# Half-swapped copies in place of the second frequency products, and a re-planned order, in a gated mixing kernel

## The chip, the cores and the metric

The kernel runs on one core of one Trainium2 chip. A core has a matrix engine (TensorE, PE in the profile; its weight loads are listed as PEld), three engines for elementwise work (VectorE or DVE, ScalarE or ACT, GpSimd or POOL), a queue engine (SP), and DMA. SBUF is the working memory, PSUM the small memory that PE writes its products to. The metric is the device time of one execution in microseconds (us); before the change it is 467.32 us, the median of three runs.

## The reference

For x of 2048 rows and 640 columns the result is a mix of two branches with a gate per row:

```python
g = sigmoid((x * gate_w).sum(-1, keepdims=True))
# a: 32 heads of 20; each row attends to itself and to 7 rows before it, 2 apart; output projection wo
a = attention(x @ wqkv) @ wo
# b: filter in the frequency plane
X = rfft2(x) * (w_r + 1j * w_i)
b = irfft2(X, s=(2048, 640))
return g * a + (1 - g) * b
```

All arithmetic is in float32.

## The kernel before, in words

Row s is stored as s = 16 p + j: partition p, chunk j (0 to 15). All even chunks need only even chunks in the attention, and all odd chunks only odd ones, since the window goes in steps of 2. So the attention has two halves (`par` 0 and 1).

The work is done in this order, as far as data and buffers force it:

1. `qkv`: eight blocks (two halves, four head groups). Operands are split into a rounded high part and a rest, and three products (high-high, high-rest, rest-high) are summed. Results go to DRAM (`qkvd`). `load_w` and `load_x` load and split the operands: ACT makes the high part, DVE or POOL the rest.
2. `fold` and `cols`: x is folded by symmetry on DVE (tiles `fx`, `fe`), part of it stored in DRAM (`fd`) and loaded again, and PE makes a transform over the 128 partitions into `zg`.
3. `attend`: for each half and head pair group, DVE multiplies keys with queries (`pr`; the queries come from a PSUM bank, `qbank`, filled by ACT) and reduces to logits `L`; ACT takes exponentials; POOL multiplies with values (`pv`); DVE reduces them to `o`, which goes to DRAM.
4. `freq`: 16 groups `g` of frequencies, three or four in flight. ACT copies columns of `zg` to `zc`; PE transforms the columns to `v` and `u`; DVE makes their sum and difference `ab`; PE turns `ab` to the rows at positive frequencies (`xa`, `xb`) and at negative ones (`xc`, `xd`). A product is complex, its real part in partitions 0 to 63 and its imaginary part in 64 to 127. `xb` and `xd` are the same numbers as `xa` and `xc` multiplied by i: the halves exchanged, one with its sign turned. They are made by a second product with another slice of the table (`mm`). ACT copies `xa`, `xb` to `X`; POOL multiplies with the weights `wp` into `P`; DVE multiplies `xc` and `xd` with theirs (`p`, `xd`) and forms sum and difference `s`; PE transforms back (`g`), and ACT writes the result into `zg`. The four x tiles of a group take the PSUM banks 3 and 4 in turn (`BX`).
5. `project_even`: for each even chunk, transposes (`oTp`), 30 products with `wo` (`woa`, `wob`), scaling with the gate on ACT (`ya`), and a store to DRAM (`ad`).
6. `spatial`: for each chunk the inverse transform (`oa`, `ob`, `ha`, `hb`), unfolded on DVE; even chunks add `ad` on POOL and go out.
7. `project_odd`: for each odd chunk the unfolding (`ye`, `y`), transposes, 30 products, and the output.

The code does not issue instructions as it goes. `Plan.record` notes each operation with its engine, and `Plan.cost` gives it a duration. `Plan.touch` finds dependences: a PSUM bank counts as one region, and two operations on a region depend on each other when one of them writes. `Plan.order` simulates all five queues many times, forward by priority and backward from due times, moves the priorities at random, and keeps the order with the smallest simulated end, averaged over draws with late loads (`late`). `Plan.issue` then issues everything in that order, so each engine's and each queue's order is fixed. Input loads get an earliest time (`op.early`), counted back from the simulated end with the constant `AHEAD`. Every recorded operation carries the line of the helper that replays it, 636, so groups are told apart by their tiles.

Of the kernel before, what the change touches and what calls it, by code (L numbers as in the profile page):

```python
# [141 lines left out]
class Op:  # L142
    __slots__ = ("i", "eng", "name", "call", "busy", "lat", "size", "preds", "succs", "chain", "tail", "start", "end", "early", "group", "of", "two")
# [12 lines left out]
class Plan:  # L156
# [31 lines left out]
    def touch(self, op, ap, write):  # L188
# [14 lines left out]
        for pg in np.unique(idx // size):  # L203
            mine = idx[idx // size == pg]
            lo, hi, dense = mine[0], mine[-1], len(mine) == mine[-1] - mine[0] + 1
            kept = []
            for acc in pages.get(pg, ()):
                o, w, q0, q1, alo, ahi, adense, aidx = acc
                hit = o is not op and q0 < p1 and p0 < q1 and alo <= hi and lo <= ahi
                if hit and not (dense and adense):  # L210
                    hit = len(np.intersect1d(mine, aidx, assume_unique=True)) > 0
                if hit and (w or write):
                    op.preds.add(o)
                covered = write and hit and p0 <= q0 and q1 <= p1
                if covered:
                    covered = lo <= alo and ahi <= hi if dense else len(np.setdiff1d(aidx, mine, assume_unique=True)) == 0
                if not covered:
                    kept.append(acc)
            kept.append((op, write, p0, p1, lo, hi, dense, mine))
            pages[pg] = kept  # L220

    def record(self, eng, name, fn, a, k):
        op = Op()
        op.i, op.eng, op.name, op.chain, op.group = len(self.ops), eng, name, self.chain, self.group
        op.preds, op.succs, op.size, op.early, op.two = set(), [], 0, False, False
# [7 lines left out]
        ins = [v for v in aps if v is not out]  # L233
# [7 lines left out]
    def cost(self, op, out, ins, k):  # L241
# [5 lines left out]
        elif op.eng == "PE":  # L247
            n = int(np.prod(out.shape[1:]))
            if op.name == "transpose":
                op.busy = 0.109  # L250
            elif ins[-1].dtype == F32R:
                op.busy = n / 2400 + 0.018
            else:
                op.busy = 4 * n / 2400 + 0.006
            op.lat = 0.25
        elif op.eng == "DVE":
            op.busy, op.lat = 0.075 + n / 960, 0.12
            two = sum(v.tensor.tag[:4] not in ("bank", "qban") for v in ins) == 2
            if op.name == "scalar_tensor_tensor":
                op.busy += 0.06  # L260
            elif op.name == "reciprocal":
                op.busy += n * 0.007
            elif two:
                op.two = True
        elif op.eng == "ACT":
            strided = any(len(v.ap) > 2 and v.ap[-1][0] > 1 for v in [out] + ins)
            op.busy, op.lat = 0.12 + n * (1.75e-3 if strided else 0.78e-3), 0.15
            if len(ins) > 1:
                op.busy += 0.1
        else:  # L270
            spread = any(v.ap[-1][0] == 0 for v in ins)
            op.busy, op.lat = 0.09 + n * (2e-3 if spread else 2.25e-3), 0.14
        if op.eng in ("DVE", "ACT", "POOL") and not op.size:
            op.busy *= PACE

    def order(self):
# [17 lines left out]
        for op in ops:  # L294
            op.early = max(0.0, span - op.tail - AHEAD) if op.early else 0.0
# [3 lines left out]
        best = self.turns(TURNS)  # L299

        names = {n: i for i, n in enumerate(dict.fromkeys(op.of for op in ops))}
        family = np.array([names[op.of] for op in ops])
        for _ in range(AGAIN):
            move = MOVE * rng.choice([0.3, 1.0, 2.0]) * rng.normal(size=len(names))
            move *= rng.random(len(names)) < rng.choice([0.1, 0.5, 1.0])
            for op, t in zip(ops, (best[1] + move[family]).tolist()):
                op.tail = t
# [21 lines left out]
    def late(self, order, draw):  # L329

        line = {e: [op for op in order if op.eng == e] for e in ENGS}
        at, free, rings, link = dict.fromkeys(ENGS, 0), dict.fromkeys(ENGS, 0.0), dict.fromkeys(ENGS, 0.0), 0.0
# [3 lines left out]
        for _ in range(len(order)):  # L336
            for e in ENGS:
                if head.get(e) is None and at[e] < len(line[e]):
                    op = line[e][at[e]]
                    t = free[e]  # L340
                    for q in op.preds:
                        if q not in out:
                            break
                        t = max(t, over[q] if q.eng == e and not q.size else out[q])
# [9 lines left out]
            if op.size:  # L354
                link = max(link, end) + op.size / RATE
                own = rings[e] = max(rings[e], end) + op.size / QUEUE
                end = (own if own >= link else min(link, own + op.size / QUEUE)) + SOONEST + LATER_BY * late
# [53 lines left out]
    def forward(self):  # L411
# [4 lines left out]
        free, rings, link = dict.fromkeys(ENGS, 0.0), dict.fromkeys(ENGS, 0.0), 0.0  # L416
# [5 lines left out]
        while len(done) < len(ops):  # L422
# [28 lines left out]
            if op.size:  # L451
                link = max(link, op.end) + op.size / RATE
                own = rings[e] = max(rings[e], op.end) + op.size / QUEUE
                avail = own if own >= link else min(link, own + op.size / QUEUE)
# [48 lines left out]
class Mixer:  # L503
# [364 lines left out]
    def freq(self, g):  # L868
# [58 lines left out]
        z, sz = col("xc", 1, 0), col("xd", 1, 1)  # L927
# [202 lines left out]

def build(tc, ins, out):
# [45 lines left out]
```

## Time and profile before

| | |
|---|---|
| median of 3 runs (lowest, highest) | 467.32 us (467.08, 467.43) |
| span of the profiled execution, first to last instruction | 465.3 us; its own time is not listed, the median is 2.0 us above the span |
| PE busy | 457.0 us, 98% of the span |
| DVE busy | 423.4 us, 91% |
| POOL busy | 323.9 us, 70% |
| ACT busy | 205.2 us, 44% |
| granted clock of PE | 1.00 in all stretches |

Busy means that an engine had an instruction under way. A group row names the tile written, the tiles read, the shapes and the count; then busy time and mean duration; then idle time of the engine before these instructions, and what ended it. A row of waits gives who waited for whom, the time in total, how often, and the longest. The chain is followed back from the last instruction, at each step to what released it. A float32 product of 321 columns is two matmul instructions in the profile.

### The profile page before, as it was taken

To read this page: it belongs to the slowest core of one execution; us is meant where nothing else is said; L and a number is where in the kernel's file an instruction comes from. 1 tells how busy PE (TensorE), PEld (TensorE's weight loads), DVE (VectorE), ACT (ScalarE), POOL (GpSimd) and SP (SyncE) were. 2 spreads that over 40 slices of the span, in tenths; PEclk is the share of its full clock that TensorE was granted. 3 is DMA by queue.
4 is the path that set the end of the run, shared out by engine and by line. 5 is a ranking of instruction groups with operands and counts; after the bars stand their busy time and mean duration, and the time that the engine had idled before them with its cause. 6 is when DMAs were issued, how large, how long until landed. Compare 5 with 4: busy or idle time off the path is not lost.

```text
span 465.3 us, 7240 instructions
## 1 busy us (share of the span) xinstructions
PE 457.0 (98%) x2497; PEld 399.5 (86%) x2497; DVE 423.4 (91%) x555; ACT 205.2 (44%) x539; POOL 323.9 (70%) x264
## 2 busy tenths in 40 slices
PE   7999999999999999999999999999999999999997
PEld 4788888888889888899887788898888999988996
DVE  4699959999999999998999999999999997989784
ACT  5523346533335453257356465545444564333110
POOL 1003847999999879988698996767877997952300
PEclk9999999999999999999999999999999999999999
DMA  8999998796877968959998466567543321447732
GB/s 310 403 376 308 393 381 314 230 299 197 242 216 252 322 187 275 282 167 276 343 258 307 135 217 220 185 183 234 182 129 120 103 80 56 136 141 220 227 113 85
DMA packets 71700, 105.90 MB, mean 228 GB/s; under 512 B 20704, under 2 KB 50400, under 8 KB 71664
## 3 DMA queue, kind: packets, MB, share of 16 engines
q1 hardware_dynamic: 40624, 69.90, 46.0%
q10 hardware_dynamic: 30128, 31.55, 20.9%
q0 software_dynamic: 912, 4.00, 2.1%
q8 instruction: 19, 0.31, 0.3%
q14 instruction: 17, 0.14, 0.1%
HBM read 72.59 MB, written 32.84 MB: 227 GB/s over the span
## 4 chain that ended last, share of the span: by engine, by line
PE 82%; DVE 10%; DMA 4%; issue 2%; ACT 0%; ACTq 0%; DVEq 0%
PE qkv L636 43%; PE wob L636 6%; PE woa L636 6%; PE z L636 4%; PE ob L636 4%; PE oa L636 4%; PE u L636 2%; PE v L636 2%; PE hb L636 2%; PE g L636 2%; PE ha L636 2%; DVE xd L636 2%; DMA fx<-in_x 2%; PE oTp L636 2%; DVE s L636 1%
## 5 line engine op out<-in xcount | busy, mean ns | idle before, releaser
L636 PE MATMUL qkv<-w,xo 128*128 128x480 f32 (+1 forms) x480 | 110.7, 384 | 0.0
L636 PE MATMUL qkv<-w,xe 128*128 128x480 f32 (+1 forms) x465 | 104.1, 382 | 1.1 <-DVE xe L636 0.7
L636 PEld LDWEIGHTS qkv<-w,xe 128*128 128x128 f32 x465 | 87.3, 188 | 17.1 <-ACT xe L636 1.8
L636 PEld LDWEIGHTS qkv<-w,xo 128*128 128x128 f32 x480 | 89.8, 189 | 13.7
L636 ACT COPY ev<-qkv 128x480 f32<-128x480 f32 x64 | 35.4, 558 | 71.9 <-PE qkv L636 60.9
L636 PE MATMUL woa<-wo,oT 128*128 128x320 f32 x240 | 51.2, 317 | 0.1
L636 PE MATMUL wob<-wo,oT 128*128 128x320 f32 x240 | 50.4, 314 | 0.0
L636 PEld LDWEIGHTS wob<-wo,oT 128*128 128x128 f32 x240 | 39.0, 188 | 0.8 <-ACT ya L636 0.2
L636 PEld LDWEIGHTS woa<-wo,oT 128*128 128x128 f32 x240 | 39.0, 188 | 0.7 <-ACT oT L636 0.4
L636 POOL TENSOR_TENSOR w<-raw,w 128x480 fp32r<-128x480 f32 (+1 forms) x20 | 28.6, 1442 | 11.1 <-ACT w L636 11.1
L636 POOL TENSOR_TENSOR P<-X,wp 128x642 f32<-128x642 f32 x16 | 25.0, 1562 | 15.4 <-ACT X L636 15.4
L636 POOL DMA_DIRECT2D fd<-fx x6 | 4.3, 717 | 37.5 <-DMA raw<-in_wqkv 31.3
L636 POOL TENSOR_TENSOR yi<-yi,y 128x640 f32<-128x640 f32 x8 | 12.4, 1558 | 20.5 <-DMA yi<-ad 14.9
L636 ACT CAST oT<-oTp 128x384 fp32r<-128x384 f32 (+1 forms) x32 | 13.1, 427 | 29.9 <-PE oTp L636 25.2
L636 PEld LDWEIGHTS g<-mm,s 128*128 128x128 f32 x150 | 21.5, 191 | 3.6 <-ACT zg L636 0.2
L636 PE MATMUL g<-mm,s 128*128 128x128 f32 x150 | 22.7, 274 | 0.0
L636 PE MATMUL oa<-gt,zg 128*128 128x161 f32 (+1 forms) x96 | 22.1, 344 | 0.0
L636 PE MATMUL u<-bt,zc 128*128 128x321 f32 (+2 forms) x96 | 22.1, 344 | 0.0
L636 PE MATMUL v<-bt,zc 128*128 128x321 f32 (+2 forms) x96 | 22.1, 344 | 0.0
L636 PE MATMUL ob<-gt,zg 128*128 128x161 f32 (+1 forms) x96 | 21.0, 344 | 0.0
L636 ACT CAST w<-raw 128x480 fp32r<-128x480 f32 (+1 forms) x30 | 17.4, 594 | 7.4 <-DMA raw<-in_wqkv 2.2
L636 PEld LDWEIGHTS v<-bt,zc 128*128 128x128 f32 x96 | 16.3, 190 | 4.0 <-ACT vs L636 0.2
(301 smaller groups left out, 1118.7 us busy)
## 6 DMA issues: line engine op xcount, KB each, us to landing
qkvd<-ev ACTq DMA_DIRECT2D x32, 480.0 KB, 4.8
wp<-in_ws SPq DMA_DIRECT2D x16, 642.0 KB, 4.4
raw<-in_wqkv SPq DMA_DIRECT2D x25, 240.0 KB, 5.8
fx<-in_x SPq DMA_DIRECT2D x8, 641.0 KB, 9.0
ot<-od SPq DMA_DIRECT2D x16, 320.0 KB, 3.4
fd<-fx POOLq DMA_DIRECT2D x6, 640.0 KB, 8.5
f<-fd SPq DMA_DIRECT2D x6, 640.0 KB, 5.5
xt<-in_xT SPq DMA_DIRECT2D x8, 320.0 KB, 6.3
```

Of the source, the lines that this page charges most:

```text
L636: p.dve.memset(w, 0.0)
```

## The change

For the groups 1 to 15 (`TURN`) the second products `xb` and `xd` are no longer made on PE. Their numbers come from the first products by two ACT copies out of PSUM, each over 64 partitions: one moves the upper half to the lower with the sign turned, one the lower half to the upper. For X they go to SBUF; for the second operand they go from one PSUM bank to the other (`xd`). Group 0, whose table has another form, stays as it was.

The planner is changed with it. The durations of PE, DVE, ACT and POOL have new constants; ACT operations that touch partitions from 64 up get 0.13 us more; a dependent operation on the same engine may start only after a short time (`SAME`), and for that reads of an earlier result are noted (`raw`). The model of DMA has one rate and no limit for a single queue. Input loads get their earliest time from their first use, less `SOON` and their transfer, in two further rounds. The random search moves tiles and kinds of operations, in 150 tries instead of 60, with another seed. So the order of the whole program is found anew. (`...` marks what is left out.)

```diff
@@ cost
-            if op.name == "transpose":
+            if op.name == "transpose" or k.get("is_transpose"):
                 op.busy = 0.109
             elif ins[-1].dtype == F32R:
-                op.busy = n / 2400 + 0.018
+                op.busy = n / 2265 + 0.006
             else:
-                op.busy = 4 * n / 2400 + 0.006
+                op.busy = max(4 * n / 2400, 0.2) + 0.006
             op.lat = 0.25
         elif op.eng == "DVE":
-            op.busy, op.lat = 0.075 + n / 960, 0.12
+            op.busy, op.lat = 0.061 + n / 960, 0.12
...
         elif op.eng == "ACT":
-            strided = any(len(v.ap) > 2 and v.ap[-1][0] > 1 for v in [out] + ins)
-            op.busy, op.lat = 0.12 + n * (1.75e-3 if strided else 0.78e-3), 0.15
+            near = any(v.tensor.tag[:4] in ("bank", "qban") for v in ins[:1])
+            op.busy, op.lat = (0.055 if near else 0.09) + n * 0.84e-3, 0.15
             if len(ins) > 1:
                 op.busy += 0.1
+            if any(v.offset >= 64 * v.ap[0][0] for v in [out] + ins):
+                op.busy += 0.13
         else:
             spread = any(v.ap[-1][0] == 0 for v in ins)
-            op.busy, op.lat = 0.09 + n * (2e-3 if spread else 2.25e-3), 0.14
-        if op.eng in ("DVE", "ACT", "POOL") and not op.size:
-            op.busy *= PACE
+            op.busy, op.lat = 0.05 + n * (1.97e-3 if spread else 2.3e-3), 0.14
@@ order
-            op.early = max(0.0, span - op.tail - AHEAD) if op.early else 0.0
+            op.input, op.early = op.early, max(0.0, span - op.tail - AHEAD) if op.early else 0.0
...
         best = self.turns(TURNS)
...
+        for _ in range(2):
+            at = {op: t for op, t, _ in best[2]}
+            for op in ops:
+                if op.input:
+                    op.early = max(1.2 * (op.chain != "first"), min(at[s] for s in op.succs) - SOON - op.size / RATE)
+            for op, t in zip(ops, best[1].tolist()):
+                op.tail = t
+            best = self.turns(TURNS)
...
@@ lag
-        return 0.0 if s.eng == op.eng and not op.size else op.lat + EDGE.get((op.eng, s.eng), 0.0)
+        if s.eng == op.eng and not op.size:
+            return SAME.get(op.eng, 0.0) if op in s.raw else 0.0
+        return op.lat + EDGE.get((op.eng, s.eng), 0.0)
@@ constants
-TURNS, AGAIN, MOVE, SEED = 6, 60, 2.0, 2
+TURNS, AGAIN, MOVE, WIDE, SEED = 6, 150, 2.0, 15.0, 4
-RATE = 380e3
-QUEUE = 250e3
-LAND = 3.2
+RATE = 390e3
+LAND = 2.8
+SOON = 12.0
-PACE = 1.02
+SAME = {"DVE": 0.1, "ACT": 0.1, "POOL": 0.05}
@@ freq
+        def turn(to, o):
+
+            A.mul(to[0:64], o[64:128], -1.0)
+            A.copy(to[64:128], o[0:64])
+
         X = self.Xr.next(f"X{g}", 2, 321)
-        for i, nm in enumerate(("xa", "xb")):
-            A.copy(X[:, i], col(nm, 0, i))
+        o = col("xa", 0, 0)
+        A.copy(X[:, 0], o)
+        if g in TURN:
+            turn(X[:, 1], o)
+        else:
+            A.copy(X[:, 1], col("xb", 0, 1))
...
-        z, sz = col("xc", 1, 0), col("xd", 1, 1)
+        z = col("xc", 1, 0)
+        if g in TURN:
+            sz = self.ps(BX, f"xd{g}")[:, 0:321]
+            turn(sz, z)
+        else:
+            sz = col("xd", 1, 1)
...
+TURN = tuple(range(1, 16))
```

More of the change, by code (lines that the diff above doesn't have):

```diff
@@ L142 @@
 class Op:
-    __slots__ = ("i", "eng", "name", "call", "busy", "lat", "size", "preds", "succs", "chain", "tail", "start", "end", "early", "group", "of", "two")
+    __slots__ = ("raw", "input", "i", "eng", "name", "call", "busy", "lat", "size", "preds", "succs", "chain", "tail", "start", "end", "early", "group", "of", "two")
 class Engine:
@@ L232, in record @@
         out = k["out"] if "out" in k else a[0]
-        ins = [v for v in aps if v is not out]
+        ins = [v for v in aps if v is not out] + [out] * (sum(v is out for v in aps) > 1)
         for v in ins:
@@ L260, in cost @@
                 op.busy += 0.06
+                op.two = two
             elif op.name == "reciprocal":
@@ L343, in late @@
                             break
-                        t = max(t, over[q] if q.eng == e and not q.size else out[q])
+                        t = max(t, over[q] + (SAME.get(e, 0.0) if q in op.raw else 0.0) if q.eng == e and not q.size else out[q])
                     else:
```

30 lines of the change are left out of this document (16 added, 14 removed).

## The prediction

> **What bounds the kernel now.** I read the page first, then a table of stretches, then the chain that ended last, then groups and waits.
>
> ```profile
> span 465.3 us, 7240 instructions
> PE 457.0 (98%) x2497; PEld 399.5 (86%) x2497; DVE 423.4 (91%) x555; ACT 205.2 (44%) x539; POOL 323.9 (70%) x264
> PE 82%; DVE 10%; DMA 4%; issue 2%; ACT 0%; ACTq 0%; DVEq 0%
> ```
>
> TensorE (PE) is busy for 98% of the span and carries 82% of the chain, so it sets the time. VectorE (DVE) stands only 33.6 us of busy time behind it. The stretches (length; busy time of PE, PEld, DVE, ACT and POOL with instruction counts; granted clock; DMA) show where each engine still has idle time:
>
> ```profile
> 0.00:20.00 20.00, 17.06 (x62) 11.67 (x63) 9.03 (x15) 9.90 (x18) 1.99 (x9) 1.00 0.93 348
> 20.00:100.00 80.00, 79.84 (x365) 68.41 (x366) 73.22 (x88) 35.12 (x87) 46.30 (x37) 1.00 0.92 332
> 100.00:380.00 280.00, 278.76 (x1535) 242.50 (x1534) 273.00 (x316) 136.06 (x376) 239.14 (x193) 1.00 0.69 217
> 380.00:440.00 60.00, 59.49 (x389) 55.35 (x388) 52.28 (x101) 21.89 (x54) 35.15 (x28) 1.00 0.49 148
> 440.00:465.30 25.30, 21.88 (x153) 21.58 (x151) 15.86 (x40) 2.26 (x6) 1.36 (x1) 1.00 0.31 112
> 241.00:353.40 112.40, 111.16 (x642) 94.31 (x642) 109.38 (x174) 59.38 (x169) 88.06 (x77) 1.00 0.63 203
> 353.40:380.00 26.60, 26.60 (x169) 24.23 (x168) 26.46 (x24) 14.85 (x39) 24.34 (x18) 1.00 0.30 86
> ```
>
> PE at full clock is never free between 20 us and 440 us by more than 1%. DVE's 41.9 us of idle time lie at the start (20.00 - 9.03 = 11.0), at the end (25.30 - 15.86 = 9.4) and in the 420 us between (6.8 + 7.0 + 7.7 = 21.5). The frequency stage, about 241 to 353 us, holds both PE (111.2 of 112.4) and DVE (109.4); ScalarE (ACT) is free there for 53.0 us. So this is a program with two machines nearly full, and what PE gives up helps only as far as DVE can be packed tighter.
>
> **The change part by part.** *The second products.* Groups 1 to 15 lose the matmuls into xb and xd. The chain (start, length, what) prices a product of two instructions:
>
> ```profile
> 282.71 0.54 PE xc L636 x2
> 285.26 0.54 PE xb L636 x2
> 287.12 0.54 PE xd L636 x2
> ```
>
> 15 x 2 x 0.54 = 16.2 us leave PE, all in the stage where PE is busy end to end. The weight loads go with them, hidden before and after. If PE stays as full as it is, the span is 465.3 - 16.2 = 449.1 us. The profiled execution's own time is not listed; the median of the runs, 467.32, is 2.0 us above its span, and I carry these 2.0 us: 451.1 us. For that, other PE work must fill the hole. It exists: the even output projections need only the attention of the even half, and part of them runs behind the stage.
>
> ```profile
> 295.38 0.54 PE xa L636 x2
> 366.35 2.20 PE woa L636 x15
> 369.64 2.21 PE wob L636 x15
> 382.76 2.21 PE woa L636 x15
> 386.60 2.20 PE wob L636 x15
> 400.56 2.20 PE woa L636 x15
> 404.40 2.20 PE wob L636 x15
> 437.68 0.55 PE oTp L636 x5
> ```
>
> With the transposes an even projection is 0.55 + 4.40 = 4.95 us; the three behind 353 us are 14.9 us of filler, and a stage that ends earlier gives the rest.
>
> *The copies.* Each group swaps one ACT copy into X for four more half-height copies: 60 new ones, 15 gone.
>
> ```profile
> L636 ACT COPY X<-xa 128x321 f32<-128x321 f32 x16 | 6.9, 428 | 5.3 <-PE xa L636 5.1
> L636 ACT COPY X<-xb 128x321 f32<-128x321 f32 x16 | 6.8, 428 | 8.8 <-PE xb L636 8.6
> L636 ACT COPY qbank<-q2a 128x160 f32<-128x160 f32 x3 | 0.9, 297 | 6.3 <-DVE pr1b L636 6.3
> L636 ACT COPY L1b<-low 1x64 f32<-1x64 f32 x1 | 0.2, 246 | 0.7 <-DVE L1b L636 0.7
> ```
>
> A copy of one partition and 64 elements takes 246 ns, one of 128 partitions and 160 elements 297: the price goes by elements, not partitions, so a half-height copy of 321 costs like a full one. No row shows a move to other partitions. Lower end 0.43 each, as X; upper end 0.56, since the changed planner's cost line adds 0.13 to operands from partition 64 up. ACT gains 60 x 0.43 - 15 x 0.43 = 19.4 us, or 60 x 0.56 - 6.4 = 27.2; against 53.0 us free in the stage that costs nothing by itself, and ACT stands at 70 to 77% there. If that cover is gone, the excess is paid in full. I take 0.43 to 0.56 as no term. ACT's queue also issues the q and vt loads, and these now stand behind up to two more copies, 1.1 us, while their attention work is held up by DVE, not by them: nothing.
>
> *The way to X and to s.* X needs, instead of two products and two copies, one product and three copies, 0.54 + 3 x 0.43 = 1.83 against 2 x 0.54 + 0.43 = 1.51 (the first copy hid behind the second product): 0.3 us later, for POOL, which has 24 us free in the stage. In front of s the second operand comes after 0.54 + 2 x 0.43 = 1.40 instead of 1.08: again 0.3 us, taken up by the four groups in flight.
>
> *The two banks.* The x products turn through two PSUM banks, with three tiles per group instead of four.
>
> ```profile
> L636 PE MATMUL xa<-ab,mm x30: 433/433/436, 241.4 to 343.3; 128*128 128x321 f32 x30
> L636 DVE TENSOR_TENSOR xd<-p,xd 128x321 f32<-128x321 f32 x16 | 7.9, 497 | 0.5
> L636 DVE TENSOR_TENSOR xd<-xd,wp 128x321 f32<-128x321 f32 x16 | 7.9, 492 | 0.5 <-PE xd L636 0.5
> L636 DVE TENSOR_TENSOR s<-P,xd 128x321 f32<-128x321 f32 x16 | 7.8, 490 | 1.4
> L636 DVE TENSOR_TENSOR s<-P,xd 128x319 f32<-128x319 f32 x16 | 7.7, 479 | 0.0
> PE xb L636 <- DVE s L636: 1.2, 3, 0.7
> ```
>
> Now xc of a group takes the bank that xd of the group before held, so a ring closes: product 0.54, two copies 0.86, the two xd steps 0.99, the two s steps 0.97, in all 3.4 us, plus one or two attention steps of 1.48 us between them on DVE: 4.9 to 6.3 us. A group now takes (343.3 - 241.4) / 15 = 6.8 us, so the ring holds back nothing; before, such waits came to 1.2 us. Term: nothing; its failure is a rival.
>
> *The order.* All five engines' orders are searched anew, with costs nearer to the rows.
>
> ```profile
> 304.45 1.40 DVE L5a L636
> 11.10 7.44 DMA fx<-in_x
> POOL fd L636 <- DMA raw<-in_wqkv: 31.3, 1, 31.3
> ACT xe L636 <- DMA fx<-in_x: 2.9, 1, 2.9
> ACT w L636 <- DMA raw<-in_wqkv: 2.2, 3, 1.3
> wp<-in_ws SPq DMA_DIRECT2D x16, 642.0 KB, 4.4
> fx<-in_x SPq DMA_DIRECT2D x8, 641.0 KB, 9.0
> ```
>
> A DVE step over 1280 elements was planned at (0.075 + 1.333) x 1.02 = 1.44 us and is now planned at 1.39; the chain shows 1.40. Input loads are planned about 12 us ahead of use instead of up to 130. They move in SP's queue behind others; landing after medians of 4 to 9 us they are still in time. At the start this can save the 2.9 us in which ACT waited for a transfer that the fx loads crowded; elsewhere it can double the 2.2 us for weights. Between -2.9 and +2.2 I take zero. The fd stores on POOL wait 31.3 us behind others' data today with nobody hurt, and have that much to give.
>
> *The sum.* PE allows 449.1. DVE loses no work: 423.4 busy, and 20.4 idle at the two ends, which are PE's first and last products and stay. For 449.1 the middle could keep only 5.3 us of its 21.5. In the one stretch where DVE was plainly the fuller engine, 353 to 380, its idle share was (26.60 - 26.46) / 26.60 = 0.5%; over 100 to 380 it was 7.0 / 280 = 2.5%. With PE now behind DVE the share should fall, but not everywhere; I take 2.0%, near the longer row, of some 405 us: 8.1. Span 423.4 + 20.4 + 8.1 = 451.9, time 453.9, say 454. By the two ends of that share (2 and 10.1 us) it is 447.8 and 455.9; the lower is under PE's 451.1 and does not count alone.
>
> **The rivals.** *PE alone decides.* DVE packs to below 1.3% idle and the time is 451.1, with the start's 2.9 us also won 448.2. For it: 0.5% has been reached; against it: only over 26.6 us, with attention alone.
>
> *DVE waits for the copies.* The two new copies out of xc's bank and the DVE multiply p, which reads the same bank, become ready together, and the planner sees no order between two readers. The qbank row above shows ACT waiting 6.3 us for a DVE reader of one shared bank. If p is held behind both copies, that is up to 15 x 0.86 = 12.9 us of DVE time on the fuller engine: up to 454 + 12.9 = 466.9, and at half of it 460.4. Against it: DVE has a queue of attention work, so p often comes after the copies anyway. The Trainium skill, "PSUM — Partial Sum Buffer", section "PSUM bank collisions raise a hardware error", says that two engines must not touch one bank and quadrant at once, two reads included, and that software has to keep them apart; by that rule this rival's wait must exist wherever the two would overlap. The trace does not contradict it, but no row before the change shows two readers.
>
> *Slower: the ring opens.* If ACT, in its fixed order, brings the copies late, or DVE puts three attention steps into each round, the group interval grows. The stage's last product and the end of PE's work (timeline of PE, and the chain):
>
> ```profile
> 352.92 0.61 PE L636 MATMUL g<-mm,s 128*128 128x128 f32 x4
> 461.92 0.55 DVE y L636
> ```
>
> Behind the last frequency product PE has 461.9 - 353.4 = 108.5 us of work, 93.6 without the three even projections, and 3.4 us follow it. The old span is reached when the stage ends at 465.3 - 3.4 - 93.6 = 368.3, that is at 6.8 + 14.9 / 15 = 7.8 us per group. At 8.3 us the stage ends at 376, span 473.1, time 475. For it: ring 6.3 plus one more step is 7.8 exactly; against it: PE waits of 1.2 us today.
>
> *No effect.* The hole is not filled, PE idles for the 16 us and the time stays at 467.3.
>
> **How the numbers follow.** Two full engines: 0.52, 450 to 458, predicted 454. PE alone: 0.18, 448 to 451. DVE waits: 0.14, 458 to 466. No effect: 0.03. Ring opens: 0.13, 469 to 480. The range 447.5 to 466 takes in the first three with the start's gain and leaves the ring and no effect out. Faster by over 0.2% (about what measuring this kernel can tell from no change): 0.52 + 0.18 + 0.14 = 0.84; within 0.2%: 0.03; slower: 0.13. Since the first three cases share a sign, one range serves them.
>
> **What would show it.** Right: PE's busy time falls by 14 to 18 us; ACT's rises by 19 to 27 us; DVE's stays within 3 us of 423 and its share of the span rises to 93 or 94%; xa's spacing is at or under 6.8 us; at most one even projection follows the first oa. Wrong: DVE waiting for ACT's xd or p for over 5 us in all; PE waiting for DVE s over 5 us; an interval above 7 us; PE idle in the first 100 us behind a raw or x load.

## The result, and the profile after

The changed kernel takes 469.92 us (median of ten executions, 467.23 to 472.42) against 467.03 us (466.64 to 468.58) for the kernel before, run beside it on the same chip: a ratio of 1.0048, 95% interval 1.0026 to 1.0069. This plan of it is half a per cent slower; 454.0 us was forecast, with a range that ended at 466. Ratios are made without the executions that lie over 1.5% above the fastest of their kernel, medians with all of them; where the two disagree below, both are given.

The profiled execution of the changed kernel took 468.93 us, with a span of 467.2. Its page, span, busy times and the shares of the chain by engine:

```profile
span 467.2 us, 7180 instructions
PE 450.1 (96%) x2437; PEld 391.6 (84%) x2437; DVE 422.3 (90%) x555; ACT 223.5 (48%) x584; POOL 319.9 (68%) x264
PE 44%; DVE 23%; ACT 3%; issue 3%; DMA 2%; POOL 1%; ACTq 0%; DVEq 0%
```

Sixty matmuls are gone and PE's busy time fell by 6.9 us, but busy time here holds slow and waiting matmuls too. For a cleaner figure I take, from the trace, the median distance from the start of one matmul to the start of the next, by kind and width, and sum it over all matmuls: that is PE's work. What is left of the span, less 6.5 us that I leave to the two ends in every run, is PE's lost time. Before: work 450.8, lost 8.0. After: work 434.1, lost 26.6. So 16.7 us of work left PE, as forecast, and 18.6 us of lost time came.

Where it came, in the table of stretches (length; busy time of PE, PEld, DVE, ACT, POOL with counts; granted clock; DMA) of after:

```profile
0.00:20.00 20.00, 17.80 (x61) 12.70 (x62) 13.06 (x21) 12.17 (x23) 2.00 (x9) 1.00 0.92 345
20.00:62.00 42.00, 42.00 (x193) 36.15 (x193) 33.90 (x52) 11.51 (x29) 11.12 (x11) 1.00 0.98 361
62.00:140.00 78.00, 78.00 (x362) 67.33 (x361) 77.03 (x67) 34.16 (x90) 70.38 (x55) 1.00 0.81 254
140.00:180.00 40.00, 34.12 (x162) 29.13 (x162) 39.15 (x36) 18.34 (x46) 33.32 (x27) 0.91 0.77 238
180.00:240.00 60.00, 59.95 (x331) 53.15 (x331) 57.34 (x49) 27.36 (x77) 54.11 (x43) 1.00 0.81 251
240.00:360.00 120.00, 114.98 (x662) 96.00 (x661) 115.06 (x180) 83.77 (x234) 93.10 (x80) 1.00 0.67 216
360.00:380.00 20.00, 20.00 (x129) 18.53 (x128) 19.90 (x18) 11.15 (x29) 19.68 (x16) 1.00 0.29 90
380.00:440.00 60.00, 59.50 (x388) 55.38 (x387) 44.67 (x87) 22.78 (x54) 36.17 (x27) 1.00 0.46 139
440.00:467.20 27.20, 23.75 (x164) 23.23 (x163) 22.20 (x53) 2.26 (x6) 0.00 (x0) 0.98 0.35 124
```

and the same stretches of before, where they differ most:

```profile
20.00:62.00 42.00, 41.84 (x190) 35.67 (x191) 38.12 (x58) 16.29 (x38) 16.89 (x14) 1.00 1.01 368
62.00:140.00 78.00, 78.00 (x360) 67.29 (x360) 74.70 (x63) 32.99 (x88) 68.66 (x54) 1.00 0.80 260
140.00:180.00 40.00, 40.00 (x220) 35.57 (x219) 38.99 (x36) 20.01 (x50) 33.75 (x27) 1.00 0.83 273
180.00:240.00 60.00, 60.00 (x320) 52.93 (x320) 57.57 (x52) 27.50 (x82) 52.75 (x42) 1.00 0.82 254
240.00:360.00 120.00, 118.76 (x687) 100.91 (x686) 116.94 (x178) 63.68 (x180) 94.72 (x81) 1.00 0.61 196
```

Two things are to be seen. First, PE's hole in 140 to 180: 162 matmuls instead of 220, a clock of 0.91. Then PE's holes in the frequency stage, 5.0 us instead of 1.2. Counted by the distances between matmuls, lost time rose by 9.4 us in the first and, between 240 and 360, by 8.5. Second, DVE. From 62 us, soon after the first attention step, to 380 it is as full in both kernels: idle 9.5 us of 318 after (0.97 + 0.85 + 2.66 + 4.94 + 0.10) and 9.9 before. Its idle time lies around that block: 15.0 us in the first 62 (before 14.9) and 20.3 behind 380 (before 17.2).

What PE waited for (engine, what it waited for, total, times, longest) says that neither of the large waits is for DVE's s or for the x products' ring:

```profile
PE qkv L649 <- ACT zg L649: 3.3, 1, 3.3
PE qkv L649 <- ACT ev L649: 2.5, 1, 2.5
PE xa L649 <- DVE ab L649: 1.8, 1, 1.8
```

ACT was late there, and not for want of time (18.3 of 40 us busy). Its line of instructions in after, up to the second stall (start, length, what, idle time before it):

```profile
162.36 0.56 ACT L649 COPY ws<-raw 128x480 f32<-128x480 f32 x1
162.37 0.38 ACTq L649 DMA_DIRECT2D qkvd<-ev  x1
164.46 0.22 ACT L649 COPY L3a<-low 1x16 f32<-1x16 f32 x1 [1.53 <-DVE L3a L649]
168.49 0.56 ACT L649 COPY ev<-qkv 128x480 f32<-128x480 f32 x1 [3.82 <-DMA qkvd<-ev]
169.58 0.37 ACT L649 COPY zg<-z 128x256 f32<-128x256 f32 x1
```

The copy that empties a qkv bank stood behind a one-partition mask copy that waited for DVE, and then waited itself 3.82 us for the store that frees its ev buffer; PE's banks stayed full behind it. The frequency stage itself had the forecast durations, product, copies and DVE steps (count, busy time, mean ns, idle time before):

```profile
L649 PE MATMUL xa<-ab,mm 128*128 128x321 f32 x30 | 10.9, 444 | 1.8 <-DVE ab L649 1.8
L649 DVE TENSOR_TENSOR p<-xc,wp 128x321 f32<-128x321 f32 x16 | 7.8, 486 | 2.7 <-ACT xd L649 2.5
L649 ACT ACTIVATE X<-xa 64x321 f32<-64x321 f32 x15 | 6.6, 437 | 6.9 <-PE xa L649 6.3 <-POOL pr5b L649 0.4
L649 ACT COPY X<-xa 64x321 f32<-64x321 f32 x15 | 6.3, 420 | 0.2
L649 ACT ACTIVATE xd<-xc 64x321 f32<-64x321 f32 x15 | 6.2, 411 | 1.8 <-PE xc L649 0.9
L649 ACT COPY xd<-xc 64x321 f32<-64x321 f32 x15 | 6.0, 399 | 4.5 <-DVE p L649 4.3
```

but it did not end earlier: it began later (first xa at 251.4 us instead of 241.4), ran at (342.6 - 251.4) / 15 = 6.1 us a group instead of 6.8, and its last g ended at 355.5 instead of 353.5. The same three even projections stand behind it (after, timeline of PE):

```profile
367.45 2.48 PE L649 MATMUL woa<-wo,oT 128*128 128x320 f32 x15
384.82 2.61 PE L649 MATMUL woa<-wo,oT 128*128 128x320 f32 x15
403.67 2.47 PE L649 MATMUL woa<-wo,oT 128*128 128x320 f32 x15
```

### The profile page after: what moved, and what is told of

Its sections match the earlier page's. It is cut to its first block, busy times and chain, and to the rows that moved or that the text cites. A ratio compares the mean times of both kernels' runs of the same rounds, so it can differ in the third digit from the quotient of the medians.

```text
span 467.2 us, 7180 instructions
## 1 busy us (share of the span) xinstructions
PE 450.1 (96%) x2437; PEld 391.6 (84%) x2437; DVE 422.3 (90%) x555; ACT 223.5 (48%) x584; POOL 319.9 (68%) x264
## 4 chain that ended last, share of the span: by engine, by line
PE 44%; DVE 23%; ACT 3%; issue 3%; DMA 2%; POOL 1%; ACTq 0%; DVEq 0%
PE qkv L649 8%; PE woa L649 7%; PE wob L649 7%; PE oa L649 4%; PE ob L649 4%; PE z L649 2%; PE hb L649 2%; PE g L649 2%; PE ha L649 2%; DVE xd L649 2%; PE u L649 2%; DMA raw<-in_wqkv 2%; PE oTp L649 1%; PE v L649 1%; PE xc L649 1%
## 5 line engine op out<-in xcount | busy, mean ns | idle before, releaser
L649 PEld LDWEIGHTS qkv<-w,xo 128*128 128x128 f32 x480 | 91.9, 193 | 21.2 <-ACT zg L649 3.8
L649 PE MATMUL qkv<-w,xe 128*128 128x480 f32 (+1 forms) x465 | 102.5, 382 | 0.4 <-DVE xe L649 0.4
L649 PE MATMUL woa<-wo,oT 128*128 128x320 f32 x240 | 49.7, 317 | 1.1 <-DVE oT L649 0.5
L649 PE MATMUL wob<-wo,oT 128*128 128x320 f32 x240 | 48.6, 314 | 0.2 <-ACT ya L649 0.2
L649 POOL TENSOR_TENSOR w<-raw,w 128x480 fp32r<-128x480 f32 (+1 forms) x20 | 25.1, 1269 | 19.2 <-ACT w L649 19.2
L649 POOL TENSOR_TENSOR P<-X,wp 128x642 f32<-128x642 f32 x16 | 25.0, 1560 | 17.2 <-ACT X L649 17.0
L649 PE MATMUL g<-mm,s 128*128 128x128 f32 x150 | 23.8, 280 | 1.1 <-DVE s L649 0.7
L649 PE MATMUL v<-bt,zc 128*128 128x321 f32 (+2 forms) x96 | 21.5, 344 | 0.0
L649 DVE TENSOR_TENSOR oT<-oTp,oT 128x384 fp32r<-128x384 f32 (+1 forms) x32 | 15.4, 483 | 4.9 <-ACT oT L649 4.8
```

What stands on the lines that cost most here:

```text
L649: p.dve.memset(w, 0.0)
```

## The experiments

The change is two changes: products become copies, and the planner is another. After the first result my theory was that DVE, full from the first attention to 380 us, sets the pace there, so that time taken from PE inside that block comes back as PE's waits. The rivals: the new planner made a bad order; the planner does not see the order of two readers of a bank; the copies cost something themselves.

### One part of the change at a time

The copies under the planner of before (the column functions of after pasted into the kernel before):

```diff
-        for i, nm in enumerate(("xa", "xb")):
-            A.copy(X[:, i], col(nm, 0, i))
+        o = col("xa", 0, 0)
+        A.copy(X[:, 0], o)
+        if g in TURN:
+            turn(X[:, 1], o)
...
+            turn(sz, z)
```

> The copies of the change alone, with the planner of before. Theory A (the copies do what they say, and the loss is the new planner's, whose DMA model puts the start of the attention too early, so that PE later waits for work that runs late): PE's work falls by 16 us, no stall of several us in the projection stage, time 455 to 462. Theory B (the copies themselves eat the gain, by the two banks and the waits between DVE and ACT): PE loses its 16 us to waits in the frequency stage, time 465 to 471.

Measured: 466.16 us (462.92 to 469.97), ratio 0.9949 (0.992 to 0.9977). The time is in the range of theory B, but its account holds only in part: of PE's lost time 11.8 us lie between 240 and 360 us (before 2.7) and 7.1 in a stall of the odd projections behind 380 (before 1.6). The new planner without the copies:

```diff
-TURN = tuple(range(1, 16))
+TURN = ()
```

> The planner of the change alone, all second products back on PE (no group is turned). Theory A: the attention again starts about 9 us later than planned and PE stalls in the projection stage, while PE has 16 us more work: 473 to 483. Theory B: the new order is as good as the old one, 464 to 469.

Measured: 480.84 us, ratio 1.0283 (1.0247 to 1.0319). So with the planner of before the copies win 0.5%, not the 3% forecast, and the new planner alone loses 2.8%. Not all of the latter has to do with order on the engines: PE's waits of this run hold one on an input load, which the new planner means to issue about 12 us ahead of use,

```profile
PE z L649 <- DMA fc<-in_t_fc: 6.4, 1, 6.4
```

which after does not have. The difference of the two kernels with the new planner, 10.9 us, is therefore no measure of the copies.

### What of the new planner

Two of its parts were put back, one at a time: the two-level model of the transfers (a rate per queue and a rate for all), and input loads issued long ahead (the loop that moves them close to use runs zero times).

```diff
-                end = link + SOONEST + LATER_BY * late
+                own = rings[e] = max(rings[e], end) + op.size / QUEUE
+                end = (own if own >= link else min(link, own + op.size / QUEUE)) + SOONEST + LATER_BY * late
...
-RATE = 390e3
-LAND = 2.8
+RATE = 380e3
+QUEUE = 250e3
+LAND = 3.2
```

> The changed kernel with one part of the planner undone: its DMA model is that of before (380 instead of 390 KB per us, a limit of 250 KB per us for each queue, landing 3.2 instead of 2.8 us). Theory A: the planned start of the attention moves towards the real one, the stall near 145 to 170 us goes, 454 to 462. Theory B: no change to speak of, 466 to 471.

```diff
-        for _ in range(2):
+        for _ in range(0):
```

> The changed kernel without the two rounds that move input loads to 12 us ahead of their use; loads keep the earliest times of before. Rival C (late loads cost the time, as the chain's 7.3 us of a weight load suggests): the stall goes, 455 to 462. Theory A: the stall stays, since the stores and loads of the attention are late and not the inputs, 464 to 471.

Measured: 474.24 us (ratio 1.0132, 1.0056 to 1.0209) and 468.65 us (1.0022, 0.9995 to 1.005). Neither part alone explains after: the first, slower than both ranges set for it, made it worse; the second is within the spread of after. Next, two readers of one bank on different engines in their order:

```diff
-                if hit and (w or write):
+                if hit and (w or write or tag[:4] == "bank" and o.eng != op.eng):
```

> The changed kernel; its planner now also keeps an order between two readers of one PSUM bank on different engines (the copies out of xc or xa and the DVE step that reads the same bank). The rival 'DVE waits for the copies': these waits, which the trace of after shows as 4.3 + 2.5 us, let plan and run drift apart; with them planned the time falls to 458 to 464 us. The theory that VectorE (DVE) is full from the first attention to about 380 us, so that the PE time given up there only turns into PE waits: no gain, 466 to 472 us, PE's lost time stays at 20 us or more.

Measured: 467.84 us, ratio 1.0004 (0.9975 to 1.0033). The waits that after has between ACT's second copy out of xc and DVE's p shrank (DVE's waits in the frequency stage of this run),

```profile
DVE p L649 <- ACT xd L649: 1.9, 4, 1.2
```

and ACT's wait for p is no longer among its larger ones, but PE's lost time stayed at 27.1 us and the time in the range of the theory. And the same kernel with another seed of the planner's search:

```diff
-TURNS, AGAIN, MOVE, WIDE, SEED = 6, 150, 2.0, 15.0, 4
+TURNS, AGAIN, MOVE, WIDE, SEED = 6, 150, 2.0, 15.0, 2
```

> The changed kernel with another seed of its planner's search (2), nothing else. It sizes what one plan differs from the next for no reason of the change: planned end 448.6 us against 448.0 of after. If after's loss against before is one unlucky plan: 455 to 462 us. If it is general: 465 to 473 us.

Measured: 464.31 us (463.67 to 465.05), ratio 0.9929 (0.9906 to 0.9951), between the two ranges. One seed moves the changed kernel by 5.6 us, from slower than before to faster. That is the size below which no single pair of plans says much, and it bounds what the following comparisons can claim.

### Take DVE's fullness away, take the copies away

The logits' reductions of the odd half were taken over half of the head dimensions only, which took 19.1 us from DVE's busy time in the kernel before (423.4 to 404.3) and 17.0 in the first run above (421.0 to 404.0):

```diff
-                in_=pr.rearrange("p j r (h d) -> p j r h d", d=HD),
+                in_=pr.rearrange("p j r (h d) -> p j r h d", d=HD)[:, :, :, :, 0 : HD // 2 if par else HD],
```

> The kernel before, with DVE's logits reductions of the odd half taken over half of the head dimensions: that part of the odd logits is left out, 32 steps of 1.40 us become about 0.7 us, 22 us of DVE work go. Theory DVE-full: before is bound by PE as well (450.8 us of work plus ends), so it stays near PE's bound, 460 to 467 us. If the kernel before is bound by DVE alone it falls to 450 us or less.

> The copies under the planner of before (the second run's partner, 466.16 us), with the same DVE reductions of the odd half taken over half of the head dimensions (that part of the odd logits is left out; 22 us less DVE work). Theory DVE-full: PE's freed 16 us can now be used, 449 to 457 us, at least 8 us under the relieved kernel before. Rival, that the copies themselves or the two-bank ring cost PE its gain: 460 to 466 us, within 3 us of the relieved kernel before.

Measured: 468.05 us and 462.18 us. Before does not move at all, so it was bound by PE, as the prediction read it. With DVE relieved the copies bring 5.9 us (468.05 to 462.18; by the ratios 6.1), without it 1.8 (467.91, before's median beside that run, to 466.16; by the ratios 2.4): more, but not the 16; 462.18 lies in the rival's 460 to 466, but not within its 3 us of the relieved kernel before. So the second products were left out with nothing in their place, with DVE full and relieved, and under both planners:

```diff
-            turn(X[:, 1], o)
...
+        G.tensor_mul(P, X[:, 0:1].broadcast_to([128, 2, 321]) if g in TURN else X, wp[:, 0:2])
...
-            turn(sz, z)
+            sz = z
```

> The planner of before; in groups 1 to 15 the second products are gone and nothing stands in their place: the second X operand is the first read again and xd is xc's own bank, so the second half of each complex product is left out of the computation, with all 60 half-height copies. Partner: the same planner with the copies, 466.16 us. Theory that VectorE is full until 380 us and PE's freed time is worth nothing there: 463 to 467 us. Rival, that the copies, their waits and the ring cost what the products gave: 455 to 460 us, since the plan ends at 454.3 us and runs of this planner without copies end some 3 us behind the plan.

> The changed kernel, planner and all, with the second products left out of groups 1 to 15 and no copies in their place (the second half of each complex product is left out of the computation). Partner: after, 469.9 us. Theory VectorE full, late from the first attention on: 464 to 469 us. Rival, copies cost it: 455 to 461 us.

> As the run with the planner of before and no second products and no copies, and with DVE's logits reductions of the odd half over half of the head dimensions as well (both parts are left out of the computation). Partner: the same with the copies, 462.2 us. If the copies and their waits are what still held that run: 452 to 457 us. If what is left is lateness of loads and order that has nothing to do with the copies: 459 to 463 us.

Measured: 461.34, 464.15 and 450.82 us. With the planner of before, medians, and PE's work and lost time in the profiled execution:

| | DVE as it is | DVE relieved |
|---|---|---|
| second products | 467.4 to 467.9 (450.8, lost 8.0) | 468.05 (450.0, lost 10.3) |
| copies | 466.16 (434.0, lost 24.6) | 462.18 (434.0, lost 19.5) |
| neither | 461.34 (433.9, lost 18.1) | 450.82 (434.0, lost 8.9) |

Leaving out 16.2 us of products is worth 17.2 us when DVE has room and 6.1 us when it has none: DVE's fullness takes two thirds of the gain, with no copy in the program. Each cell is one plan, and 5.6 us lie between two seeds; the 11.1 us between these two gains are twice that. The copies then take 4.8 us more with DVE full and 11.4 us with DVE relieved (by the ratios 3.4 and 10.8). Under the new planner the copies take 5.8 us (469.92 to 464.15). Each theory explains a part, and with the planner of before neither number that I had set for one of them alone (463 and up; 460 and under) was met; under the new planner 464.15 is in the range of the theory that DVE is full, and 450.82 lies below both ranges set for it. The stretches of the two runs without products and copies, DVE as it is:

```profile
62.00:240.00 178.00, 178.00 (x895) 155.76 (x894) 170.63 (x147) 80.84 (x216) 155.85 (x123) 1.00 0.83 262
240.00:345.00 105.00, 99.66 (x599) 85.51 (x598) 102.33 (x169) 54.89 (x156) 80.88 (x73) 1.00 0.69 219
345.00:440.00 95.00, 93.15 (x600) 86.35 (x600) 90.60 (x139) 37.05 (x96) 67.10 (x50) 1.00 0.45 137
```

and relieved:

```profile
62.00:240.00 178.00, 178.00 (x899) 156.04 (x898) 170.55 (x156) 81.55 (x222) 163.07 (x129) 1.00 0.84 266
240.00:345.00 105.00, 104.40 (x640) 91.05 (x639) 101.97 (x175) 58.52 (x167) 90.22 (x78) 1.00 0.68 217
345.00:440.00 95.00, 94.05 (x617) 88.38 (x617) 78.86 (x150) 33.75 (x84) 50.88 (x39) 1.00 0.42 132
```

Between 240 and 345 both have DVE at 102 us of 105, but the relieved one gets 640 matmuls through PE and the other 599, and 175 DVE steps instead of 169.

Not all of the 4.8 and 11.4 us is the copies' own. PE's lost time by stretch, in the profiled executions:

| | 140 to 240 us | 240 to 360 | 380 to 440 |
|---|---|---|---|
| copies, DVE as it is | 0.1 | 11.8 | 7.1 |
| neither, DVE as it is | 0.1 | 8.7 | 3.3 |
| copies, DVE relieved | 5.2 | 6.7 | 2.1 |
| neither, DVE relieved | -0.1 | 2.0 | 2.0 |
| after | 9.7 | 11.1 | 1.6 |
| after, neither | 9.7 | 5.7 | 1.7 |

Between 240 and 360 us, where the copies are made, they add 3.1, 4.7 and 5.5 us of lost time (before rounding). The rest comes mostly from stalls of PE where no copy is made. With DVE relieved it is in the main one stall near 175 us, 70 us before the first copy: an ACT copy into qbank waited for DVE, and the ev copy that frees PE's bank stood behind it.

```profile
PE z L636 <- ACT ev L636: 3.0, 1, 3.0
174.61 0.30 ACT L636 COPY qbank<-q3b 128x160 f32<-128x160 f32 x1 [3.71 <-DVE pr3a L636]
```

And the 9.7 us that after loses between 140 and 240 us are lost by its plan without copies too, in part by other waits.

### Which part of the copies costs

All with DVE relieved and the planner of before, between 450.82 (neither) and 462.18 us (all copies). The same number of copies on ACT, but inside SBUF and read by nobody (the line stands in both places); only the pair into X; only the pair into xd's bank (in the first and the third of these runs POOL again reads the first half of X twice):

```diff
+            turn(X[:, 1], X[:, 0])
```

> VectorE relieved, planner of before, second products and exchanging copies left out (450.82 us); now ACT does 60 half-height copies of the same size in the same places of its queue, from X's first half to its second, inside SBUF, which nobody reads (the second half of each complex product and half of the odd logits stay out of the computation). If ACT's occupancy is what the copies cost (11.4 us between 450.82 and 462.18): 458 to 463 us. If it is the longer way through the PSUM bank to X and s: 450 to 453 us.

```diff
-            turn(sz, z)
+            sz = z
```

> As the relieved run with all copies (462.18 us), but only the pair from xa into X is made; the pair from xc into xd, with what it adds to the product, is left out of the computation, as is half of the odd logits. If the way to s (xc, two copies, then DVE) is the costly one: 451 to 454 us. If the way to X or ACT's occupancy by number of copies: 456 to 461 us.

```diff
-            turn(X[:, 1], o)
```

> As the relieved run with all copies (462.18 us), but only the pair from xc into xd's bank is made; the pair into X is left out of the computation, as is half of the odd logits. If the way to s with the bank kept longer is the costly one: 457 to 462 us. If it is the way to X: 451 to 454 us; if ACT's occupancy by number: 456 us or so here and in the run with the X pair.

Measured: 453.96, 453.61 and 456.51 us: 3.1, 2.8 and 5.7 us over the run without copies. The first and the third lie just outside the ranges set for them. PE's lost time between 240 and 360 us was 4.9, 3.0 and 6.9 us, against 2.0 without copies and 6.7 with all. By that stretch the way through xc's bank to s costs most, as much as all copies together, and copies that carry nothing cost some as well. In the third run DVE waits for the copies, as it does with all copies (2.0 us there), and not in the other two:

```profile
DVE p L636 <- ACT xd L636: 3.4, 8, 0.8
```

The Trainium skill, "PSUM — Partial Sum Buffer", section "PSUM bank collisions raise a hardware error", says that two engines must not read one bank and quadrant at once, so that software has to put one behind the other. The waits between ACT's xd and DVE's p, 4.3 and 2.5 us in after and 3.4 here, fit it. But that run also has three tiles of a group in the two banks, where the other two have two, and what this does was not separated from the waits. Since 5.6 us lie between two seeds, not even the order of the three is shown by their times; and the 11.4 us of all copies, the one number far from theirs, holds the stall near 175 us.

### A plan with slack, and what it is worth

DVE's start times in the trace can be set against those in the kernel's own plan. How many us DVE is behind the plan:

| | at 64 us | at 240 | at 340 | plan's end |
|---|---|---|---|---|
| before | 2.9 | 2.5 | 3.6 | 463.3 |
| copies, planner of before | 5.5 | 5.5 | 9.5 | 454.5 |
| neither, planner of before | 6.9 | 3.6 | 5.7 | 454.3 |
| after | 9.2 | 12.5 | 19.7 | 448.0 |
| after, other seed | 5.4 | 6.3 | 13.7 | 448.6 |
| after, neither | 9.6 | 13.5 | 15.9 | 446.2 |

Between 240 and 340 us DVE falls 1.1 to 2.4 us further behind in the plans without copies and 4.0 to 7.4 in those with them. In after 9.2 us are lost at the first attention step already and never come back; before, whose plan gave a DVE step of 1280 elements 1.44 us where it takes 1.40, falls no further behind up to 240. So the planner of after was given later transfers and longer steps (with the bank readers' order of the run above, and seed 3, the one of five whose plan ended first):

```diff
-DRAWS, SOONEST, LATER_BY = 3, 2.4, 0.6
+DRAWS, SOONEST, LATER_BY = 3, 4.3999999999999995, 0.6
...
-LAND = 2.8
+LAND = 4.8
...
-SAME = {"DVE": 0.1, "ACT": 0.1, "POOL": 0.05}
+SAME = {"DVE": 0.17, "ACT": 0.1, "POOL": 0.05}
...
+        if op.eng in ("DVE", "ACT", "POOL") and not op.size:
+            op.busy *= 1.01
```

> The full changed kernel under after's planner with durations made later rather than shorter: transfers land 4.8 us after their last byte is planned in place of 2.8, a DVE step that reads its neighbour's output waits 0.17 us in place of 0.1, all DVE, ACT and POOL steps are 1% longer, two readers of one bank keep their order, seed 3. Its plan ends at 460.6 us, after's at 448.0. If lateness against the plan is what cost after its gain: the run ends within 5 us of this plan, 460 to 465 us, faster than both kernels. If not: 467 to 473 us.

> The planner and seed of the run that came to 462.15 us, with all second products kept and no copies. Its plan ends at 468.4 us (460.6 with the copies). If the change itself brings the gain once the plan has slack: 468 to 474 us. If the planner alone does: 460 to 464 us.

Measured: 462.15 us with the copies, ratio 0.9877 (0.9856 to 0.9898), and 469.09 us with the products, ratio 1.0057 (1.0026 to 1.0088). Faster than both kernels, and by 6.9 us the change's own. But a plan's luck can be as large, so the pair was run again with seed 2:

> The full changed kernel under the slacker planner with seed 2 in place of 3 (plan's end 462.2 us). If the gain is the change's: 461 to 466 us. If seed 3 was luck: 467 us or more.

> The same planner and seed 2 with all second products kept and no copies (plan's end 469.8 us). If the change is worth some 7 us under this planner: 468 to 474 us. If the pair with seed 3 owed it to its plans: within 3 us of the run with the copies.

Measured: 468.94 us with the copies, in executions from 461.30 to 472.66, and 469.48 us (469.03 to 469.77) with the products; by the ratios 0.9931 (0.9887 to 0.9976) and 1.0027 (1.0011 to 1.0042). By medians the copies win next to nothing in this pair, by ratios 1%, and that ratio rests on three of the ten executions with the copies. The 462.15 us of seed 3 were partly luck. In the same planner, seed and search, the copies were worth 1.8 us (planner of before), 6.9 and 0.5: from next to nothing to less than half of the 16.2 us of products. The 10.9 us under the planner of after are no fourth value, because of the load wait of 6.4 us in the partner.

## Why the prediction was wrong

**What bounds the kernel.** Right: before does not move when DVE is relieved (468.05), and loses its 17.2 us when the products go and DVE has room (450.82). "Two machines nearly full" held too.

**Products off PE, 16.2 us.** Right: PE's work fell by 16.7 us.

**"Other PE work must fill the hole. It exists: the even output projections."** This failed. Three of them stood behind the last g before, and three stand there after. They exist, but nothing in after brings the last g forward (its end is at 353.5 us before, 355.5 after): what stands before it is DVE's attention work, the same in both kernels. In other plans it comes forward by part of the 16 us: to 350.8 with the other seed, 348.2 with the copies under the planner of before, 345.2 there with neither; and to 337.4 only with neither and DVE relieved.

**The sum, by DVE's idle share.** This is the step that gave the number, and it failed. I let the idle time of DVE's middle, 20 to 440 us, fall from 21.5 to 8.1 us; it rose to 32.9 (8.1 in 20 to 62, 9.5 in 62 to 380, 15.3 in 380 to 440). A mean over 420 us hid that DVE's block from 62 to 380 had only 9.9 us of idle time to give, already 3%, and that the rest lay around the start of the attention, where DVE waits for ACT's copy into qbank (8.1 us in after, 4.2 before), and in the tail, where PE is full and DVE idles behind it. The ends had 11.9 (6.9 + 5.0) instead of the 20.4 that I had left as they were; 8.5 us thus only changed places, 4.0 at the start, where DVE did some work earlier and waited later, and 4.4 at the end, where it did work later. 422.3 + 11.9 + 32.9 = 467.1, the span. The one experiment that gave DVE room and made no copies got the whole gain.

**The copies at no cost.** Their price was at or just under the lower end (399 to 437 ns forecast as 0.43 to 0.56 us, ACT up 18.3 us against 19.4 to 27.2), and that ACT has room was right; that this makes them free was wrong: whole runs are 4.8 us longer with DVE full and 11.4 with DVE relieved, of which 3.1 and 4.7 us of lost time lie in the copies' stage. I had priced the later X and s at 0.3 us each, "taken up by the four groups in flight".

**The two banks.** Right: 6.1 us a group, no wait of weight on the ring in after. With the planner of before xa waited 2.5 us once for an xd copy.

**The order, taken as zero.** Wrong, and unsettled in its parts. With the copies in both, after is 3.8 us slower than the run under the planner of before; with another seed it would have been 1.9 us faster. I bounded it by input loads only (-2.9 to +2.2); the load wait of 6.4 us in the run without copies is outside even that. The stall between 140 and 180 us, 9.4 us of the 18.6 us of lost time that came, belongs here: the same planner loses as much there without copies.

**The rivals.** "DVE waits for the copies" exists, at 2.5 us in after instead of up to 12.9, and planning for it changed nothing. "The ring opens", the slower rival, has the right side but not the mechanism: 6.1 us a group in the mean, and single intervals of xa up to 9.3 us where before has them up to 11.5. "No effect", to which I gave 0.03, says that the hole is not filled and PE idles: that is nearest to what happened. Of the signs I had named as showing the prediction wrong, two appeared, but before has them as well: xa intervals above 7 us, and PE idle behind an x load (0.8 us, before 0.9). Of those that would show it right, most failed: PE's busy time fell by 6.9 us, not 14 to 18, ACT's rose by 18.3, not 19 to 27, DVE's share is 90, not 93%, and three projections, not one, follow the first oa. DVE's busy time and the spacing of xa came as named.

**What stays open.** The sizes of the two causes rest on one plan each, and what the copies cost by DVE's waits, by ACT's queue and by the banks was not separated. Why one seed's plan loses 5.6 us less than another's was not taken apart, nor how much of the 3.8 us to the planner of before is such luck. That a plan which starts the attention earlier, or moves attention steps behind the frequency stage where DVE idles 15 us, would win the rest was not tried.

## What to carry to other kernels

Before adding up what a faster engine gives, look at the second engine stretch by stretch: its idle time counts only where the freed work could be put, and an average over the span hides that all of it lies in the first and last stage. To learn whether the saving is real at all, leave the work out without a substitute, once as it is and once with the second engine relieved; here those two runs differ by 10.5 us, and with them the full second engine shows as a cause of its own, apart from the copies. A searched order with accurate durations is not a safer one: two seeds of it lay 5.6 us apart, more than the change itself was worth in two of three pairs.

## What the runs showed of the hardware

PE's granted clock falls after a stall, and the loss outlasts it. In after, around its two stalls, in pieces of 4 us:

```profile
143.00:147.00 4.00, 1.47 (x10) 1.21 (x10) 4.00 (x4) 1.97 (x6) 4.00 (x5) 1.00 0.71 172
147.00:151.00 4.00, 4.00 (x19) 3.17 (x18) 4.00 (x4) 1.66 (x5) 4.00 (x5) 1.00 0.92 300
166.00:170.00 4.00, 0.65 (x3) 0.22 (x2) 3.82 (x5) 1.47 (x4) 2.71 (x3) 0.90 1.11 361
170.00:174.00 4.00, 4.00 (x10) 3.37 (x11) 4.00 (x5) 1.94 (x6) 1.26 (x2) 0.50 1.04 387
174.00:178.00 4.00, 4.00 (x15) 3.36 (x15) 3.96 (x5) 1.54 (x3) 4.00 (x3) 0.75 0.43 111
```

The first stall, 2.5 us, leaves the clock at 1.00; the second, 3.35 us, is followed by 4 us at 0.50 and 4 at 0.75. A stall of 3.0 us in the relieved run with copies was followed by a stretch at 0.66. From the chain of after, 28 qkv matmuls took 9.11 us behind the second stall and 117 took 25.50 later, 0.218 each: 9.11 - 28 x 0.218 = 3.0 us, nearly as much again as the stall.

```profile
170.00 9.11 PE qkv L649 x28
184.03 25.50 PE qkv L649 x117
```

The Trainium skill, "TensorE: Matmul & The Clock Gate", section "HAM oscillation — how this bites in real kernels", sets the bound at gaps of about 3.4 us; these runs do not bear out a bound on the single gap. In the copies' run under the planner of before, two gaps of 0.57 and 2.46 us with 0.85 us of matmuls between were followed by 4 us at 0.50; in the slack plan with copies and seed 2, one gap of 2.05 us was followed by 3.4 us at 0.51; and 2.68 us in the run with neither under the planner of before, like the 2.5 us in after, left the clock at 1.00. In that order, each gap's end and the stretch behind it:

```profile
420.23 1.43 PE L636 MATMUL woa<-wo,oT 128*128 128x320 f32 x4 [2.46 <-DVE oT L636]
421.00:425.00 4.00, 4.00 (x18) 3.89 (x17) 2.75 (x7) 0.85 (x2) 0.00 (x0) 0.50 0.30 102
140.86 0.46 PE L651 MATMUL z<-fc,fx 128*128 128x128 f32 x2 [2.05 <-DMA fc<-in_t_fc]
142.00:145.40 3.40, 2.81 (x14) 2.51 (x13) 3.40 (x3) 2.96 (x9) 3.40 (x4) 0.51 0.72 242
252.63 0.78 PE L636 MATMUL xa<-ab,mm 128*128 128x321 f32 x2 [2.68 <-DVE ab L636]
253.00:257.00 4.00, 4.00 (x26) 3.43 (x24) 3.88 (x8) 2.36 (x7) 4.00 (x4) 1.00 0.67 239
```

So the length of one gap alone did not decide it here; what did was not worked out. The clock also differs between repeated executions of one program: with the copies under the planner of before, 462.92 us came with a mean granted clock of 1.000 and 469.97 with 0.984, and 1.6% of 465 us is 7.4 us, about the difference. Ten executions of the kernel before spread by 1.9 us, ten of the copies with slack and seed 2 by 11.4 (clock 0.999 in the fastest, 0.984 in the slowest; 1.5% of 468 us is 7.0 us, so not all of it is the clock). I had expected an engine with spare time to be harmless; in after, spare time on PE that was gathered into the second gap cost nearly twice its length.
